# A chunked scan joined to a gated feed-forward layer: a new order for the scan of the last three chunks, the sums for the seven products, and own tiles for the last rows

## The chip, the cores and the metric

One core of a Trainium2 chip runs the whole kernel in one launch. The metric is device time in microseconds (us), the median of repeated executions. TensorE (PE) multiplies matrices, with its weight loads (PEld) shown apart; VectorE (DVE), ScalarE (ACT) and GpSimd (POOL) work element by element; SyncE (SP) issues most DMA transfers. Each engine works through its own list of instructions in order; semaphores are all that ties one list to another.

## The reference, cut to what matters

```python
# x (4, 8, 768, 32), a (4, 8, 768), B and C (4, 8, 768, 16); float32
for c in chunks:                                   # state-space scan
    cum = cumsum(log(clip(a)))
    M = (C @ B.T) * exp(cum_i - cum_j) * causal
    y = M @ x + (C @ state) * exp(cum)
    state = exp(sum(log a)) * state + sum_j B_j x_j exp(cum_last - cum_j)
z = y.transpose(0, 2, 1, 3).reshape(3072, 256)     # all heads side by side
gate = sigmoid(z @ w_gate)                         # 256 x 1536
out = (gate * (z @ w_val)) @ w_out                 # 1536 x 256
```

The kernel walks the sequence in six chunks of 128 positions. The 512 rows of `z` that belong to one chunk (four batches) go through the feed-forward layer as soon as the scan has made them.

## The kernel before, in words

Products in single precision are made of three products of rounded parts: an operand is cast to a high part, and the difference to the operand is the low part. So every operand costs a cast (mostly ACT) and a subtraction (mostly POOL or DVE), named hi and lo below.

For chunks 0 to 3 the feed-forward layer runs as `gateK_f` and `valueK_f` (K the chunk, f one of 12 strips): six matmuls of 128x512 each (line 1244) into PSUM tiles `pg` and `pv`, a sigmoid on ACT, a multiplication on DVE (line 1205), then hi (line 1209) and lo (line 1211). `projK` (line 1500) multiplies by the output weights, in two column halves 0 and 1. Three PSUM banks serve all of these.

Chunks 4 and 5 are joined. Their rows and the weights are cut in two by two blocks, and seven products stand for eight (the "scheme of seven products"). It needs sums of rows (`x_block`: names b11, b21, b22, t1 to t4) and, for each of 12 weight tiles, sums of weights (`s_block`, s0 to s11: one sum `ww`, four sums `sw`, hi, lo). `group` i does the seven products (line 1365, 3 matmuls each, tiles gva, gvb, gvd). `corner` takes them out of PSUM (copy on ACT, line 1398; sums on DVE, line 1400; sigmoid; multiplication, lines 1391 and 1407). `h_parts` makes hi (line 1417) and lo (line 1419) of the result. `out` multiplies by the output weights (line 1441). `stored_rows` copies and stores the results (lines 1455 and 1457).

The scan of chunks 2 to 5 runs in ten pieces, `block0` to `block9`, that lie between the steps of the feed-forward layer on PE. A block makes the part across chunks for one half of the batches, the products of B and C for a later half, and the part within the chunk for the half between. After a block, ACT copies the banks (`inner`), DVE weighs the products (`weights`), adds (`result`) and forms the states (`after`); the next block needs these.

What stands where is written out by hand: `ORDER` is a list of steps, each an engine and a task, and `run` issues exactly that list, so it sets the order on each engine. A step's needs are only tested against that list; they do not move anything.

Of the kernel before, what the change touches and what calls it, by code (L numbers as in the profile page):

```python
# [88 lines left out]
pool.value2_2 sp.x4_2 dve.value2_3 pe.gate2_4 sp.b5_2 dve.after3_2 sp.p4_0 act.value2_3 dve.after3_2
pe.value2_4 act.gate2_4 pool.value2_3 sp.a5_2 dve.value2_4 pe.gate2_5 dve.turn4_2 act.value2_4 pe.value2_5  # L90
act.gate2_5 pool.value2_4 sp.t5_0 act.turn4_2 dve.value2_5 pe.gate2_6 act.value2_5 pe.value2_6 act.gate2_6
pool.value2_5 pool.before4_0 dve.value2_6 pe.gate2_7 sp.p4_2 dve.decays5_2 act.value2_6 sp.a5_3 pe.value2_7
act.gate2_7 pool.value2_6 dve.value2_7 pe.gate2_8 dve.turn5_0 act.value2_7 pe.value2_8 act.gate2_8
pool.value2_7 sp.t5_2 act.turn5_0 dve.value2_8 pe.gate2_9 dve.decays5_3 act.value2_8 pe.value2_9 act.gate2_9
pool.value2_8 dve.value2_9 pe.gate2_10 act.value2_9 pe.value2_10 act.gate2_10 pool.value2_9 pe.block5
dve.value2_10 act.value2_10 pool.value2_10 pe.gate2_11 act.inner4_0 dve.weights4_2 sp.x5_0 pool.before4_2
dve.after4_0 dve.weights4_2 pool.decays5_0 act.gate2_11 pe.value2_11 dve.result3_2 pool.decays5_1 dve.after4_0
act.result3_2 dve.turn5_2 pool.result3_2 pe.proj2_0 dve.after4_0 act.turn5_2 dve.value2_11 dve.after4_0
act.value2_11 dve.result3_2 pe.proj2_1 dve.after4_0 pool.value2_11 act.result3_2 dve.after4_0 sp.p5_0
pool.result3_2 pe.proj2_0 pe.proj2_1 pe.proj2_0 pe.proj2_1 dve.proj2_0 pe.gate3_0 dve.proj2_1 sp.proj2_1  # L100
# [12 lines left out]
act.xb22_1 pe.block8 dve.xb22_0 pool.xb22_1 dve.value3_11 dve.value3_11 pe.proj3_0 dve.result5_0
pool.value3_11 act.inner5_2 dve.result5_0 dve.xb11_0 pool.xt1_0 act.xb21_0 pe.proj3_0 dve.xb11_0 dve.xb21_0
pool.xt2_0 act.xt1_0 dve.xt1_0 pe.proj3_1 act.xt2_0 dve.xt4_0 pool.xt3_1 dve.xt2_0 act.xt4_0 dve.xt4_0 pool.s0
act.xt3_1 pe.proj3_1 dve.xt3_1 dve.after5_2 dve.after5_2 dve.after5_2 dve.s0 pe.block9 pe.proj3_0
dve.result5_2 act.s0 dve.result5_2 pe.proj3_0 dve.xb11_1 pool.s0 act.xb21_1 dve.xb11_1 dve.xb21_1 pe.proj3_1
dve.xt1_1 dve.xt2_1 act.xt1_1 dve.xt2_1 pool.xt4_1 dve.xt2_1 pe.proj3_1 dve.xt1_1 act.xt4_1 dve.xt4_1 dve.s1
pool.s2 pe.group0 dve.s1 pe.group0 act.corner0_11 pe.group0 act.s1 dve.s2 pe.group0 act.corner0_22 dve.s1
act.corner0_21 pe.group0 dve.corner0_11 pool.s3 act.s2 pe.proj3_0 dve.corner0_21 act.corner0_11 dve.s2  # L120
act.corner0_21 pe.group0 dve.s3 pe.proj3_0 dve.corner0_22 act.s3 dve.proj3_0 pe.group0 act.corner0_22 pool.s3
pe.group1 act.corner0_12 pe.group1 act.corner1_11 pe.group1 act.corner1_22 pe.group1 dve.corner1_11 pe.group1
act.corner1_21 dve.corner1_11 pe.proj3_1 dve.corner1_21 dve.corner1_21 pe.group1 pe.proj3_1 dve.corner1_22
dve.corner1_22 pe.group1 act.part0_11 dve.proj3_1 pool.s4 pe.group2 act.part0_22 pe.group2 dve.part0_11
# [74 lines left out]
def tile_ssd_then_gated_ffn(  # L199
# [1109 lines left out]
    def s_block(i):  # L1309
# [4 lines left out]
        if i == 0:  # L1314
            needs += [("py", 2 * T1 + 1)]
# [532 lines left out]
```

## Time and profile before

| | |
|---|---|
| median of 3 runs | 366.8 us (365.11 to 366.99) |
| the profiled execution | 366.27 us |
| its span, first to last instruction | 364.5 us |
| PE busy | 346.8 us, 95% of the span |
| DVE, ACT, POOL busy | 241.2, 168.3, 178.0 us |
| granted TensorE clock, mean | 0.998 |

The profiled execution is 1.77 us longer than its span. A busy PE is not a PE at its peak, since the ends of matmuls are modelled: the pace is better read from the distance between the starts of like steps. The feed-forward layers of chunks 1 to 3 and the blocks of the scan take PE from about 88 to 235 us, the joined chunks from there to the end.

### The profile page before, as it was taken

The numbers are of one execution on the slowest core, as the hardware profiler recorded it, in microseconds if no ns is written. First come the engines' busy times: TensorE is split into PE (matmuls) and PEld (weight loads), VectorE is DVE, ScalarE is ACT, GpSimd is POOL, SyncE is SP. The second block draws the span as 40 slices with busy tenths as digits, with TensorE's granted clock in tenths as the row PEclk, the third lists the DMA queues.
The fourth block names the chain that finished last, engine by engine and source line by source line (L and its number), as shares of the span: only waits on it lengthen the run. The fifth ranks groups of instructions, "written<-read, shape, count | busy, mean of one in ns | idle before, by whom it ended". The sixth has DMA issues, their size and how long they took to land.

```text
span 364.5 us, 8267 instructions
## 1 busy us (share of the span) xinstructions
PE 346.8 (95%) x3328; PEld 277.5 (76%) x3328; DVE 241.2 (66%) x425; ACT 168.3 (46%) x315; POOL 178.0 (49%) x174
## 2 busy tenths in 40 slices
PE   8999999999999999999999999978999798999993
PEld 3567477787888888888888888856788686888883
DVE  7787688776428775545611234789798979666473
ACT  2585784356875410555310443323646363534521
POOL 6444875746898642456520454455415656313030
PEclk9999999999999999999999999999999999999999
DMA  7999964445364434253200210000011000000003
GB/s 166 242 231 212 335 185 134 107 84 94 107 117 127 80 84 90 58 101 103 45 14 13 49 30 12 8 0 2 1 32 28 0 0 2 0 2 0 0 2 115
DMA packets 87467, 27.43 MB, mean 75 GB/s; under 512 B 75718, under 2 KB 80262, under 8 KB 87430
## 3 DMA queue, kind: packets, MB, share of 16 engines
q1 hardware_dynamic: 82982, 26.26, 30.4%
q10 hardware_dynamic: 4448, 0.66, 1.1%
q8 instruction: 26, 0.43, 0.5%
q14 instruction: 11, 0.09, 0.1%
HBM read 23.46 MB, written 3.44 MB: 74 GB/s over the span
## 4 chain that ended last, share of the span: by engine, by line
PE 63%; DVE 18%; DMA 5%; SPq 4%; issue 3%; ACT 1%; POOL 0%; DVEq 0%; POOLq 0%
PE pg L1244 13%; PE pv L1244 13%; PE po L1500 10%; PE po L1538 6%; PE acc L1441 5%; PE gva L1365 4%; DVE c L1400 3%; DVE c L1407 3%; PE gvb L1365 3%; DVE h L1417 2%; PE gvd L1365 2%; DMA a_z<-a 2%; DMA wr<-in_moe_w_val_dram 2%; SPq L418 2%; PE banks L784 1%
## 5 line engine op out<-in xcount | busy, mean ns | idle before, releaser
L1211 POOL TENSOR_TENSOR h<-g,h 128x512 fp32r<-128x512 f32 x36 | 48.8, 1357 | 57.4 <-ACT h L1209 55.6
L1244 PE MATMUL pg<-xh,w 128*128 128x512 f32 x168 | 59.6, 395 | 0.0
L1244 PE MATMUL pv<-xh,w 128*128 128x512 f32 x168 | 58.9, 391 | 0.1
L1205 DVE TENSOR_TENSOR g<-pv,g 128x512 f32<-128x512 f32 x36 | 24.8, 689 | 40.4 <-PE pv L1244 39.2
L1500 PE MATMUL po<-h,w 128*128 128x512 f32 x216 | 50.9, 391 | 0.0
L1500 PEld LDWEIGHTS po<-h,w 128*128 128x128 f32 x216 | 40.3, 188 | 8.6
L1441 PEld LDWEIGHTS acc<-w,h 128*128 128x128 f32 x288 | 38.7, 190 | 3.4 <-DVE h L1419 0.4
L1441 PE MATMUL acc<-w,h 128*128 128x256 f32 x288 | 40.0, 283 | 0.2 <-DVE h L1419 0.2
L1419 POOL TENSOR_TENSOR h<-c,h 128x512 fp32r<-128x512 f32 x11 | 19.0, 1741 | 43.2 <-ACT h L1417 29.7
L1184 ACT ACTIVATE g<-pg 128x512 f32<-128x512 f32 x44 | 26.3, 598 | 29.3 <-PE pg L1244 28.9
L1209 ACT CAST h<-g 128x512 fp32r<-128x512 f32 x35 | 21.7, 619 | 37.9 <-DVE g L1205 37.9
L1244 PEld LDWEIGHTS pg<-xh,w 128*128 128x128 f32 x168 | 31.5, 188 | 7.9 <-DVE h L1201 0.8
L1244 PEld LDWEIGHTS pv<-xh,w 128*128 128x128 f32 x168 | 31.5, 188 | 7.2 <-POOL w L496 0.6
L1244 PE MATMUL pg<-xl,w 128*128 128x512 f32 x84 | 32.7, 390 | 0.0
L1244 PE MATMUL pv<-xl,w 128*128 128x512 f32 x84 | 32.7, 389 | 0.0
L574 DVE TENSOR_TENSOR_SCAN ab<-ab,delta 128x512 f32<-128x512 f32 x20 | 28.0, 1403 | 4.1 <-DMA ab<-a_z 4.1
L496 POOL TENSOR_TENSOR w<-wr,w 128x512 fp32r<-128x512 f32 x18 | 26.7, 1485 | 7.8 <-ACT w L494 7.0
L477 POOL TENSOR_TENSOR wr<-wr 128x512 int32<-128x512 int32 x18 | 20.4, 1138 | 12.6 <-ACT wr L475 7.7
L1538 PE MATMUL po<-wr,h 128*128 128x256 f32 x96 | 23.4, 394 | 0.1
L1332 POOL TENSOR_TENSOR s<-sw,s 128x512 fp32r<-128x512 f32 x8 | 10.8, 1362 | 22.8 <-ACT s L1330 22.8
L1538 PEld LDWEIGHTS po<-wr,h 128*128 128x128 f32 x96 | 17.6, 188 | 4.3 <-DVE h L1201 0.6
L1400 DVE TENSOR_TENSOR c<-gva,c 128x512 f32<-128x512 f32 x12 | 8.3, 690 | 18.8 <-PE gva L1365 18.7
(194 smaller groups left out, 669.2 us busy)
## 6 DMA issues: line engine op xcount, KB each, us to landing
ab<-a_z SPq DMA_DIRECT2D x40, 128.0 KB
wr<-in_moe_w_gate_dram SPq DMA_DIRECT2D x6, 512.0 KB
wr<-in_moe_w_val_dram SPq DMA_DIRECT2D x6, 512.0 KB
wr<-in_moe_w_out_dram SPq DMA_DIRECT2D x6, 512.0 KB
xn<-in_x_dram SPq DMA_DIRECT2D x10, 256.0 KB
out_dram<-o SPq DMA_DIRECT2D x48, 32.0 KB
bn<-in_B_dram SPq DMA_DIRECT2D x10, 128.0 KB
out_dram<-o SPq DMA_DIRECT2D x10, 128.0 KB
```

The source lines that it names most:

```text
L477: nc.gpsimd.tensor_tensor(out=lw.bitcast(I32), in0=hw.bitcast(I32), in1=lw.bitcast(I32), op=ALU.add)
L496: engines[eng].tensor_tensor(out=lo, in0=lw, in1=hi.bitcast(F32), op=ALU.subtract)
L574: nc.vector.tensor_tensor_scan(out=t.rearrange("p h l -> p (h l)"), data0=t.rearrange("p h l -> p (h l)"), data1=delta.rearrange("p h l -> ...
L1184: nc.scalar.activation(gs[k, f], pm, AF.Sigmoid)
L1205: nc.vector.tensor_tensor(out=g, in0=pm, in1=g, op=ALU.mult)
L1209: copies[eng](hh, g)
L1211: engines[eng].tensor_tensor(out=hl, in0=g, in1=hh.bitcast(F32), op=ALU.subtract)
L1244: nc.tensor.matmul(pm, w[:, part, kt, fs], xx[:, kt], start=(i == 0), stop=(i == 3 * NK - 1))
L1365: nc.tensor.matmul(out, one, two, start=m == 0 and n in (1, 7, 2), stop=m == 2, skip_group_check=True)
L1441: nc.tensor.matmul(acc[:, k * DM : (k + 1) * DM], one(js), w[:, two, :], start=first and m == k == 0, stop=final and m == 2, skip_group_ch ...
L1500: nc.tensor.matmul(acc, w[:, part], hs[k, f][:, of_h], start=(f == 0 and i == 0), stop=(f == NF - 1 and i == 2))
L1538: nc.tensor.matmul(acc[:, :DM], hs[k, f][:, js], whole[NF + f // 2][:, f % 2], start=start, stop=stop, skip_group_check=True,)
```

## The change

`ORDER` is new from the middle of chunk 1 on. Blocks 2 to 9 stand earlier: block 6 moves from chunk 3's strips into those of chunk 2, block 7 to their end, and blocks 8 and 9 from the joined chunks' stage into `proj2`. The sums of x for t1 to t4 follow in `proj2` and at the start of chunk 3; b22 and s0 to s3 stand within chunk 3's strips; s4 to s7 during `proj3` and `group0`. Four weight sums, s8 to s11, stay among the groups. In `h_parts` the cast is always on ACT. `proj3` takes strips 8 to 11 first, which sets free the tiles that s4 to s7 use. The last four rows of chunk 5 get two more buffers, of the tag "cd". No arithmetic is added or taken away; the number of PE instructions is the same.

```diff
 ORDER = """
...
-pe.gate3_10 act.value3_9 pe.value3_10 act.gate3_10 pool.value3_9 dve.value3_10 pe.gate3_11 dve.after5_0
+pe.proj2_1 pool.xt1_0 pool.xt2_0 act.xt1_0 pool.xt1_0 act.xt2_0 pool.xt2_0 pe.block9 pe.proj2_0 pool.xt4_0
...
@@ x_block
-        needs += [("gv", T2 - 1)] if MOVING_LAST[name] else []
+        needs += {"b1": [("gv", T2 - 1), ("t1", 0)], "b2": []}.get(name[:2] if name != "b21" else "b1", [("gv", T2 - 2)] if name in ("t1", "t2") else [])
...
@@ s_block
-        needs = [("w", i), ("gv", T2 - 1)] + ([("s7", i - 2)] if i > 1 else [])
...
-        needs += {0: moved if v else [], 1: moved, 2: [("proj", T2 - 1)], 3: [("proj", T2 - 1)], 4: [("done", 1)], 5: [("done", 2)]}[j]
+        needs = [("w", i)] + ([("sums", i - 1)] if i else [])
+        needs += {
+            0: [("py", 2 * T1 + 1)], 1: [("py", 2 * T1 + 1)], 2: moved, 3: moved, 4: [("projf", 8)], 5: [("projf", 8)],
+            6: [("projf", 10)], 7: [("projf", 10)], 8: [("done", 2)], 9: [("done", 3)], 10: [("done", 4)], 11: [("done", 5)],
+        }[i]
...
@@ h_parts
-        eng = yield step(("act", "dve"), (ACT_SB, DVE_MM), [("hf", j, n)] + ([("hused", j - 2, n)] if j > 1 else [("proj", T2 - 1)]))
+        eng = yield step("act", ACT_SB, [("hf", j, n)] + ([("hused", j - 2, n)] if j > 1 else [("proj", T2 - 1)]))
...
@@ stored_rows
-            pool, tag = (wk, "o") if k == T1 else (ld, ("bn", "pp")[at])
+            pool, tag = (wk, ("o", "cd")[at]) if k == T1 else (ld, ("bn", "pp")[at])
...
@@ proj_turned
-        for n in range(0, NF, size):
+        starts = [*range(8, NF, 2), *range(0, 8, 2)] if size == 2 else [*range(0, NF, 4)]
+        for n in starts:
...
-                        acc, w[:, part], hs[k, f][:, of_h], start=(f == 0 and i == 0), stop=(f == NF - 1 and i == 2)
+                        acc, w[:, part], hs[k, f][:, of_h], start=f == starts[0] and i == 0,
+                        stop=f == starts[-1] + size - 1 and i == 2,
```

On PE, block 9 before (the eight rows with `banks` and `local`) stands within `proj3`, after strips 0 to 3 of both halves (`po_0`, `po_1`; `h_3` and `h_4` are strips):

```order
L1500 MATMUL po_1_3129<-h_3_2679,w_1269 128x512 x3
L814 MATMUL banks<-cd_2_2983,sn_2865 64x64 x3
L814 MATMUL local<-cd_2_2983,sn_2865 64x64
L814 MATMUL banks<-cd_2_2983,sn_2865 64x64 x3
L814 MATMUL local<-cd_2_2983,sn_2865 64x64
L814 MATMUL banks<-cd_2_2983,sm_3157 64x64 x3
L814 MATMUL local<-cd_2_2983,sm_3157 64x64
L814 MATMUL banks<-cd_2_2983,sm_3157 64x64 x3
L814 MATMUL local<-cd_2_2983,sm_3157 64x64
L1500 MATMUL po_0_3098<-h_4_2699,w_1358 128x512 x3
```

In the changed kernel the same block, at its new line, stands within `proj2`, between strips 7 and 8, with chunk 3's strips still to come:

```order
L1506 MATMUL po_1_2715<-h_7_2495,w_1399 128x512 x3
L815 MATMUL banks<-cd_2_2700,sn_2530 64x64 x3
L815 MATMUL local<-cd_2_2700,sn_2530 64x64
L815 MATMUL banks<-cd_2_2700,sn_2530 64x64 x3
L815 MATMUL local<-cd_2_2700,sn_2530 64x64
L815 MATMUL banks<-cd_2_2700,sm_2811 64x64 x3
L815 MATMUL local<-cd_2_2700,sm_2811 64x64
L815 MATMUL banks<-cd_2_2700,sm_2811 64x64 x3
L815 MATMUL local<-cd_2_2700,sm_2811 64x64
L1506 MATMUL po_0_2684<-h_8_2544,w_1452 128x512 x3
```

So the block moved ahead of twelve strips of chunk 3 and of all of `proj3`.

On DVE, this is what stands before between the weight sums of s6 and the next ones, at the end of group 3 (`c2` and `c3` are the corners of groups 2 and 3, `h1` the second pair's result):

```order
L1400 TENSOR_TENSOR c3_11_3483<-gva_3234,c3_11_3483 128x512
L1407 TENSOR_TENSOR c2_11_3392<-c3_11_3483,c2_11_3392 128x512
L1400 TENSOR_TENSOR c3_21_3508<-gvd_3235,c3_21_3508 128x512
L1407 TENSOR_TENSOR c2_21_3421<-c3_21_3508,c2_21_3421 128x512
L1400 TENSOR_TENSOR c3_22_3491<-gvb_3236,c3_22_3491 128x512
L1407 TENSOR_TENSOR c2_22_3402<-c3_22_3491,c2_22_3402 128x512
L1417 CAST h1_22_3545<-c2_22_3402 128x512
L1419 TENSOR_TENSOR h1_22_3545<-c2_22_3402,h1_22_3545 128x512
L1391 TENSOR_TENSOR c2_12_3473<-gvb_3236,c2_12_3473 128x512
L1417 CAST h1_12_3568<-c2_12_3473 128x512
L1419 TENSOR_TENSOR h1_12_3568<-c2_12_3473,h1_12_3568 128x512
```

The changed kernel has this at the same place, after the sums of s8:

```order
L1404 TENSOR_TENSOR c3_11_3501<-gva_3290,c3_11_3501 128x512
L1411 TENSOR_TENSOR c2_11_3428<-c3_11_3501,c2_11_3428 128x512
L1404 TENSOR_TENSOR c3_21_3530<-gvd_3291,c3_21_3530 128x512
L1404 TENSOR_TENSOR c3_22_3514<-gvb_3292,c3_22_3514 128x512
L1411 TENSOR_TENSOR c2_22_3438<-c3_22_3514,c2_22_3438 128x512
L1423 TENSOR_TENSOR h1_11_3543<-c2_11_3428,h1_11_3543 128x512
L1423 TENSOR_TENSOR h1_22_3569<-c2_22_3438,h1_22_3569 128x512
L1395 TENSOR_TENSOR c2_12_3494<-gvb_3292,c2_12_3494 128x512
L1423 TENSOR_TENSOR h1_12_3590<-c2_12_3494,h1_12_3590 128x512
```

Both casts went to ACT and the multiplication of corner 21 to POOL; the lo of part 11 came from POOL to DVE.

On POOL, this piece of chunk 3's strips before holds nothing but the strips' own lo (`h_4`, `h_5`, `h_6`) and the scan's small products:

```order
L1211 TENSOR_TENSOR h_4_2699<-g_4_2688,h_4_2699 128x512
L1211 TENSOR_TENSOR h_5_2792<-g_5_2708,h_5_2792 128x512
L584 TENSOR_TENSOR bd_2_2808<-bn_1_2182,ab_2_2201 128x128
L584 TENSOR_TENSOR bd_3_2811<-bn_1_2182,ab_3_2273 128x128
L856 TENSOR_TENSOR cd_0_2822<-bct_0_2294,pp_0_2524 128x256
L1211 TENSOR_TENSOR h_6_2839<-g_6_2824,h_6_2839 128x512
```

In the changed kernel chunk 3's strips on POOL have weight sums (`ww`), a lo of weight sums (`s_1`) and the lo of b22 (`xb`) among them:

```order
L1212 TENSOR_TENSOR h_3_3014<-g_3_3001,h_3_3014 128x512
L1297 TENSOR_TENSOR xb_3016<-y_0_2243,xb_3016 128x2x2x64
L1297 TENSOR_TENSOR xb_3016<-y_2_2506,xb_3016 128x2x2x64
L1212 TENSOR_TENSOR h_4_3040<-g_4_3027,h_4_3040 128x512
L1324 TENSOR_TENSOR ww_3061<-w_1101 128x512
L1212 TENSOR_TENSOR h_5_3063<-g_5_3050,h_5_3063 128x512
L1212 TENSOR_TENSOR h_6_3088<-g_6_3072,h_6_3088 128x512
L1336 TENSOR_TENSOR s_1_3110<-sw_3083,s_0_3100 128x512
L1212 TENSOR_TENSOR h_7_3112<-g_7_3097,h_7_3112 128x512
```

The scan's small products moved to chunk 2 and before, and larger work took their place.

## Rows read from the trace of the kernel before

**Rows 1.** Busy time by stretch: start:end, length, then each engine's busy us.

```profile
88.00:125.20 37.20, 37.20 (x434) 30.41 (x434) 21.82 (x34) 25.32 (x43) 29.47 (x23) 1.00 0.53 110
...
234.70:262.10 27.40, 23.29 (x232) 18.30 (x232) 24.59 (x54) 10.70 (x22) 13.03 (x13) 1.00 0.01 1
262.10:313.00 50.90, 47.19 (x259) 40.56 (x258) 43.81 (x78) 26.31 (x46) 25.99 (x18) 1.00 0.05 11
313.00:345.50 32.50, 31.65 (x181) 27.46 (x181) 20.41 (x28) 14.39 (x25) 6.94 (x4) 1.00 0.00 1
345.50:358.90 13.40, 13.03 (x88) 11.45 (x86) 9.69 (x13) 3.59 (x8) 3.54 (x2) 1.00 0.04 14
```

**Rows 2.** Waits of PE: us in total, times, the longest in us.

```profile
PE gvb L1365 <- DVE c L1391: 4.1, 4, 1.8
PE local L814 <- DVE ml L676: 2.4, 1, 2.4
```

**Rows 3.** Timeline of PE from 236 to 266: start, length, engine, line, work.

```profile
236.21 5.73 PE L1500 MATMUL po<-h,w 128*128 128x512 f32 x24
241.87 0.34 PE L814 MATMUL banks<-cd,sn 32*64 32x64 f32 x6
244.57 0.27 PE L814 MATMUL local<-cd,sn 32*64 32x64 f32 x1 [2.36 <-DVE ml L676]
...
245.36 5.76 PE L1500 MATMUL po<-h,w 128*128 128x512 f32 x24
...
252.99 0.84 PE L1365 MATMUL gva<-xt,s 128*128 128x512 f32 x3
255.28 0.96 PE L1365 MATMUL gvd<-xt,w 128*128 128x512 f32 x3 [1.44 <-ACT c L1398]
...
264.17 1.52 PE L1500 MATMUL po<-h,w 128*128 128x512 f32 x6
265.53 0.84 PE L1365 MATMUL gvb<-xt,s 128*128 128x512 f32 x3
```

**Rows 4.** Timeline of PE where group 3 ends and group 4 begins.

```profile
281.62 1.59 PE L1441 MATMUL acc<-w,h 128*128 128x256 f32 x12
283.04 0.95 PE L1365 MATMUL gvb<-xb,s 128*128 128x512 f32 x3
...
285.19 0.87 PE L1441 MATMUL acc<-w,h 128*128 128x256 f32 x6
287.84 0.96 PE L1365 MATMUL gvb<-x,w 128*128 128x512 f32 x3 [1.78 <-DVE c L1391]
```

**Rows 5.** Timeline of DVE, at 236 us and where group 3 ends.

```profile
236.94 0.43 DVE L1209 CAST h<-g 128x512 fp32r<-128x512 f32 x1
...
284.11 1.40 DVE L1417 CAST h<-c 128x512 fp32r<-128x512 f32 x1
285.54 1.65 DVE L1419 TENSOR_TENSOR h<-c,h 128x512 fp32r<-128x512 f32 x1
287.11 0.68 DVE L1391 TENSOR_TENSOR c<-gvb,c 128x512 f32<-128x512 f32 x1
```

**Rows 6.** Timeline of POOL over the same place.

```profile
281.77 3.45 POOL L1419 TENSOR_TENSOR h<-c,h 128x512 fp32r<-128x512 f32 x2
285.19 3.13 POOL L1320 TENSOR_TENSOR ww<-w 128x512 f32<-128x512 f32 x2
```

**Rows 7.** A strip of chunk 3: PE's last product and POOL's lo.

```profile
231.74 0.39 PE L1244 MATMUL pv<-xh,w 128*128 128x512 f32 x1
```

**Rows 8.** Timeline of POOL, the lo of that strip.

```profile
233.66 1.29 POOL L1211 TENSOR_TENSOR h<-g,h 128x512 fp32r<-128x512 f32 x1 [1.43 <-ACT h L1209]
```

**Rows 9.** Timeline of all engines at the end.

```profile
352.92 5.97 PE L1441 MATMUL acc<-w,h 128*128 128x256 f32 x46 [0.22 <-DVE h L1419]
...
358.67 0.36 ACTq L1457 DMA_DIRECT2D out_dram<-o  x1
...
361.37 0.42 DVE L1455 COPY o<-acc 128x256 f32<-128x256 f32 x1 [2.01 <-DMA out_dram<-o]
```

More of the change, by code (lines that the diff above doesn't have):

```diff
@@ L153 @@
+pe.out3_21 pe.group9 dve.corner9_22 pe.group10 dve.corner9_12 pool.part4_21 act.part4_22 pe.group10
+act.corner10_11 pe.out4_11 dve.part4_22 act.part4_12 pe.group10 act.corner10_22 dve.part4_12 pe.group10
 dve.corner10_11 pe.group10 act.corner10_11 pe.out4_11 act.corner10_21 pe.group10 dve.corner10_21 pe.out4_22
@@ L1267, in x_block @@
         needs = [("sum", p) for p in ((p2,) if name in ("b22", "t3") else (p1,))]
-        needs += [("gv", T2 - 1)] if MOVING_LAST[name] else []
+        needs += {"b1": [("gv", T2 - 1), ("t1", 0)], "b2": []}.get(name[:2] if name != "b21" else "b1", [("gv", T2 - 2)] if name in ("t1", "t2") else [])
+        if name == "b22":
+            needs.append(("out", T2 - 2))
+        if name == "t3":
+            needs += [("pcd", 2 * T1), ("pcd", 2 * T1 + 1)]
         if name in ("t1", "t3"):
@@ L1283, in x_block @@
             needs = []
-        eng = yield step(("act", "dve"), (ACT_HALF, DVE_HALF), needs)
+        eng = yield step(("act", "dve"), (ACT_HALF, DVE_HALF), needs, port=True)
         src = sums(name) if name[0] == "t" else (y2 if name == "b22" else y1)(int(name[1] == "2"))
@@ L1320, in s_block @@
         engines[eng].tensor_tensor(out=ww, in0=w[:, 0].bitcast(F32), in1=w[:, 1].bitcast(F32), op=ALU.add)
-        yield step("dve", 4 * 0.28, port=True)
+        yield step("dve", 4 * 0.28, [("s7", i - 1)] if i else [], [("sums", i)], port=True)
         t = ld.tile([P, 4, P], F32, tag="ab", name=f"sw{i}", bufs=NDEC)
@@ L1355, in group @@
                 needs += [("sum", 2 * T1 + 1), ("pfirst", 2 * T1 + 1)]
-            made = [("p", n, i)] + ([("done", i // 2)] if n == (4 if i == NF - 1 else 3) and i % 2 else [])
+            made = [("p", n, i)] + ([("done", i)] if n == (4 if i == NF - 1 else 3) else [])
             yield step("pe", 3 * 0.227, needs, made, port=12)
@@ L1488, in proj_turned @@
         size = 2 if k + 1 in JOINED else 4
-        for n in range(0, NF, size):
+        starts = [*range(8, NF, 2), *range(0, 8, 2)] if size == 2 else [*range(0, NF, 4)]
+        for n in starts:
             some = range(n, n + size)
-            needs = [("h", k, f) for f in some] + sorted({("w", NF + f // 2) for f in some}) + ([] if n else [("gv", k)])
-            yield step(
-                "pe", size * 3 * 0.227, needs, [("proj", k)] if mt and n + size == NF else [], port=24, banks=int(n == 0)
-            )
-            if n == 0:
+            needs = [("h", k, f) for f in some] + sorted({("w", NF + f // 2) for f in some})
+            needs += [("gv", k)] if n == 0 and size == 4 else []
+            makes = [("projf", n)] if mt and size == 2 else []
+            makes += [("proj", k)] if mt and n == starts[-1] else []
+            yield step("pe", size * 3 * 0.227, needs, makes, port=24, banks=int(n == starts[0]))
+            if n == starts[0]:
                 acc = ps_mm.tile([P, 512], F32, tag="mm", name=f"po{k}_{mt}")
```

186 lines of the change are left out of this document (91 added, 95 removed).

## The prediction, made before the run

> **What bounds the kernel now.** I read the busy time by stretch first, then the waits of PE, then the timelines around the longest of these waits. PE sets the pace from 88 us on. In the strips of chunk 1 it is busy for all of 37.20 us, with two blocks of the scan among them. After 234.70, where the last strip of chunk 3 ends, it idles 4.11 us of 27.40, then 3.71 of 50.90, 0.85 of 32.50 and 0.37 of 13.40, 9.04 in sum [rows 1]. So what an order can win lies in the joined chunks, and the reader is to see who ends those waits. The two longest entries name DVE [rows 2]. DVE is busy for 24.59 of 27.40 us and 43.81 of 50.90 in the two stretches with much waiting, and for 20.41 of 32.50 in the one with little [rows 1]. DVE's timeline shows why it is so full: a cast that takes 0.43 us at 236.94 takes 1.40 at 284.11, and a subtraction after it 1.65 [rows 5], while POOL works without a break from 281.77 to 288.32 [rows 6]. The two slow each other where both work on SBUF alone.
>
> **The change part by part.** PE's instructions stay the same, so I count lost time from start to start, which also holds PE's slow start after a stop.
>
> Block 9 waits within proj3: its first matmuls start at 241.87, the next at 244.57, so 2.7 us are lost to one small multiplication (ml) queued on DVE behind the sums of x [rows 3]. That block moves into proj2, where no sums of x stand on DVE. Gain 2.7.
>
> In group 0 the fourth product starts at 252.99. A product of three matmuls takes half of what six of the same shape take, (265.53 - 264.17) / 2 = 0.68, so the next could start at 253.67; it starts at 255.28 [rows 3]. Loss 1.6, from x and weight sums made on the spot. A third stop in this stretch is 4.11 - 2.36 - 1.44 = 0.3 [rows 1, 3]. With x's sums and s0 to s3 done in chunk 3's strips, both go: 1.9.
>
> At the ends of groups 1, 3, 5, 7 and 9 the third product of the next group needs a bank that DVE frees with the corner's multiplication (line 1391). At group 3 the last two output steps take 1.42, so 0.71 each; the step at 285.19 is over at 285.90, the product starts at 287.84, a loss of 1.9 [rows 4] of which 1.8 is told as wait. The four such waits are 4.1 [rows 2], and all idling between 262.10 and 345.50 is 3.71 + 0.85 = 4.6 [rows 1]. With some 0.15 us (1.94 - 1.78) of slow start at each of about six stops, 5.5 is lost here. At the end of group 3 DVE spends 1.40 + 1.65 on a cast and a subtraction before it reaches that multiplication at 287.11 [rows 5]. Now both casts are on ACT, and four weight sums instead of eight lie among the groups. What stays, by the new order and the rows' lengths: from the product that DVE's last sum needs to the product that waits, PE has two output steps, three products and an output step, 2 x 0.71 + 3 x 0.68 + 0.71 = 4.2. In that time DVE has the sum, one multiplication, two subtractions and the corner's multiplication, 5 x 0.68 = 3.4. That leaves 0.8, so one collision with an operation of POOL (1.29, [rows 8]) costs 0.5 and two cost 1.8. I take 0.3 at the end of group 1, where a transposition of proj3 stands in between, 0.4 at 3 and 5, where POOL works too, and nothing at 7 and 9, where the corner's multiplication comes ahead of the subtractions: 1.1 stays, between 0 and 5.5. Gain 4.4.
>
> In the last two pairs' end PE idles 0.37 [rows 1], with slow starts some 0.6; the casts of the last parts leave DVE. I take 0.4 of it.
>
> After the last matmul: PE ends at 352.92 + 5.97 = 358.89. The last copy starts at 361.37 behind the landing of an earlier store, since four rows share two buffers, and ends at 361.79; from there 2.7 us pass to the end of the span at 364.50 [rows 9]. With own buffers ACT goes on from its store at 358.67: that store 0.36, a copy 0.42, a store 0.36, a copy 0.42, so the last copy ends at 360.23 [rows 9], 1.6 earlier. If the stores' landing, and not the last copy, sets the end, the gain is less, down to 0.5.
>
> Now what is added. First, proj3 begins with strips 8 and 9 and asks for strip 11 after two steps of 1.36, 2.7 us. In a strip of chunk 3 PE starts its last product at 231.74, so is free 0.23 later at 231.97 (a sixth of 1.36), and POOL ends the lo at 233.66 + 1.29 = 234.95 [rows 7, 8]: 3.0 later. Before, strips 0 to 7 came first and hid that. Cost 0.3 to 1.6 (one more POOL operation in front); I take 0.4.
>
> Second, eight blocks (2 to 9) now ask for their inputs earlier, and DVE's scans and transpositions, and the loads on SP's queue, move with them. The cover is that blocks 1 and 2 stand among strips without any idle PE [rows 1], and that before only one block shows a wait [rows 2]. In the new order the closest pair is blocks 7 and 8, two steps of proj2 apart, 24 matmuls, which took 241.87 - 236.21 = 5.7 us [rows 3], in which DVE has two weighings, two results and three small operations, some 4 us by rows like 0.68 [rows 5]. The price lies between 0 and 2.7 per block, 21.6 in all; nearest to the rows is 0, and I take 0.4 in all. The new sums are queued behind these on DVE and POOL and are needed much later.
>
> Third, POOL in chunk 3's strips (12 x 2.72 = 32.6 us): eleven lo of 1.29, four more operations of that size and five of half size, 14.2 + 5.2 + 3.8 = 23.2 us [rows 8], 71%. In chunk 1's strips POOL is busy 29.47 of 37.20, 79%, and PE never waits [rows 1]. DVE adds three subtractions of 0.68 and sixteen small sums there. Cost 0 to 3, taken as 0.3. s4 to s7 between proj3's steps and group 0: 0 to 2, taken as 0.3.
>
> The sum: 2.7 + 1.9 + 4.4 + 0.4 + 1.6 - 0.4 - 0.4 - 0.3 - 0.3 = 9.6. From the profiled execution's own 366.27 that gives 356.7. The median of the runs lies 0.5 above it, so I predict 357.0 (range of this case 351 to 361).
>
> A rule of the Trainium skill speaks against a part of this. "SBUF — State Buffer", section "Who interferes with whom", says that a DVE operation with two SBUF inputs, or a cast in a two-port mode, and a GpSimd operation that reads SBUF shut each other out for a whole instruction, whoever starts first. The trace agrees in kind (1.40 for 0.43, above). By that rule the subtractions that came to DVE can each wait for a whole operation of POOL, at any of the five ends of groups; what that would give is the first rival.
>
> **The rivals.** (1) The ends of groups stay slow. The lo of part 11 came to DVE and the multiplication of corner 21 to POOL, so two collisions can still fall into each of these ends, and s4 to s7 run against POOL's lo of x. Then the 4.4 is not won and s4 to s7 cost 1 more: 357.0 + 4.4 = 361.4, with a part of it some 360.5. For it: 1.65 for a subtraction [rows 5]. Against: POOL has fewer operations there, and the stretch without weight sums loses only 0.85 in 32.50 [rows 1].
>
> (2) Slower: the pulled-ahead scan makes PE wait at each block, because `inner`, `weights` and `after` of one block must be through before the next, now at closer distance, with value multiplications in between. Place: PE's `banks` and `local` in chunks 1 and 2. At block 9's price of 2.7 for eight blocks it costs 21.6, of which 0.4 is in the sum already: 357.0 + 21.2 = 378. From (9.8 + 1.8) / 8, about 1.5 us per block, the kernel is slower by more than 0.5%; a centre is 372. For it: that one price was paid [rows 3]. Against: it was paid where DVE was full, and DVE is busy 21.82 of 37.20 where two blocks wait for nothing [rows 1].
>
> (3) No gain: the waits only move, since DVE, POOL and ACT have the same work in all. The 9.04 of idling then reappears in proj2, chunk 3's strips or group 0: about 366 with the own buffers' 1.6 partly kept. Against: chunk 3's strips have free DVE time.
>
> **How the numbers follow.** The forecast has 0.62, rival (1) 0.21, rival (2) 0.10, rival (3) 0.07. A measurement of this kernel tells about 0.5%, 1.8 us, from no change. Faster by more than that (under 365.0): 0.62 + 0.21 = 0.83; within it: 0.07; slower: 0.10. The range runs from 351.0 (all of 2.7 + 1.9 + 5.5 + 0.6 + 1.6, with no cost, and 3 x (32.50 - 0.85 - 2 x (14 x 0.68 + 8 x 0.71)) = 3.8, what three such stretches lose beyond their steps and stops [rows 1]) to 364.8: it takes in rival (1) and leaves out (2), (3) and the rare better case, under 0.2.
>
> **What would show it.** Right: PE without idle time from 88 us past the last strip of chunk 3; `local` without a wait for ml; group 0 without a stop; line 1391's four waits (now at 1395) together under 1.5; no DVE cast in the parts of the last stage; last copy within 1.5 us of the last matmul. Wrong: waits of `banks` for `m` or `y`, `pg` or `pv` waiting for ACT or DVE in chunk 3, or stops at every second group end as long as before.

## The result: 356.05 us against 366.83, and the profile after

The changed kernel takes 356.05 us (median of six runs, 355.48 to 356.60), the kernel before 366.83 in the same comparison; the ratio is 0.9714, 95% interval 0.9693 to 0.9735. The forecast was 357.0, range 351.0 to 364.8. The profiled execution takes 356.60 us, its span 354.7, the granted clock 0.998.

Where the 9.8 us of span went is best read from starts that both traces have. "Step of group i" is the time from its second product (tile gvd, first written) to that of the next group.

| stretch of PE | before | changed | gain | by the prediction's terms |
|---|---|---|---|---|
| span's start to block 1's first `local` | 94.82 | 95.77 | -0.95 | 0 |
| from there to group 0's first product | 156.13 | 154.20 | 1.93 | 2.7 - 0.4 - 0.4 - 0.3 = 1.6 |
| step of group 0 | 9.82 | 7.48 | 2.34 | 1.9 - 0.3 = 1.6 |
| steps of groups 2, 4, 6, 8, 10 (group 1's end, and so on) | 45.07 | 40.22 | 4.85 | 4.4 |
| steps of groups 1, 3, 5, 7, 9 | 38.31 | 38.23 | 0.08 | 0 |
| from group 11's second product to the last matmul's end | 14.06 | 13.97 | 0.09 | 0.4 |
| from there to the span's end | 5.61 | 4.15 | 1.46 | 1.6 |

The first row is not the change: that stretch took 94.67 to 97.24 us in the thirteen traces of this study. From block 1 on the gain is 10.75, which fits the medians (366.83 - 356.05 = 10.8).

Busy time by stretch of the changed kernel (columns as in [rows 1]); the last three lines are the joined chunks without their end:

```profile
88.00:125.20 37.20, 36.32 (x458) 29.08 (x457) 26.79 (x40) 24.32 (x44) 28.59 (x26) 1.00 0.59 127
206.40:239.00 32.60, 32.60 (x145) 26.99 (x145) 15.94 (x32) 16.59 (x29) 21.08 (x19) 1.00 0.08 17
239.00:266.00 27.00, 27.00 (x121) 22.36 (x120) 20.11 (x37) 11.66 (x22) 6.04 (x7) 1.00 0.00 1
266.00:313.00 47.00, 46.35 (x268) 40.49 (x268) 32.32 (x57) 27.41 (x47) 15.87 (x11) 1.00 0.06 12
313.00:347.00 34.00, 33.86 (x205) 29.98 (x203) 19.23 (x29) 17.11 (x30) 4.13 (x3) 1.00 0.00 1
```

Chunk 3's strips carry the sums without any idle PE, with DVE and POOL at 49% and 65%. `proj3` and group 0 have none either. What idles is 0.65 + 0.14 us in the joined chunks, and 0.88 in chunk 1, which was fully busy before. The waits of PE say who ends these (as in [rows 2]; from 88 us on):

```profile
PE pg L1245 <- DVE g L1206: 0.9, 1, 0.9
...
PE gvb L1369 <- DVE c L1395: 0.6, 2, 0.4
...
PE acc L1445 <- DVE h L1423: 0.2, 1, 0.2
```

`local` no longer waits, and the four waits of 4.1 in all are two of 0.6 in all. Both are at the ends of groups 3 and 5. (Before, the four lie at the ends of groups 3, 5, 7 and 9; the end of group 1, which the prediction counts too, has none.) PE there, for [rows 4]:

```profile
281.42 0.84 PE L1369 MATMUL gvd<-xt,s 128*128 128x512 f32 x3
282.10 0.87 PE L1445 MATMUL acc<-w,h 128*128 128x256 f32 x6
283.35 0.96 PE L1369 MATMUL gvb<-x,w 128*128 128x512 f32 x3 [0.37 <-DVE c L1395]
```

DVE and POOL there, for [rows 5, 6]:

```profile
280.31 2.38 DVE L1423 TENSOR_TENSOR h<-c,h 128x512 fp32r<-128x512 f32 x2
282.61 0.68 DVE L1395 TENSOR_TENSOR c<-gvb,c 128x512 f32<-128x512 f32 x1
```

```profile
280.57 1.57 POOL L1423 TENSOR_TENSOR h<-c,h 128x512 fp32r<-128x512 f32 x1 [0.73 <-ACT h L1421]
282.10 1.73 POOL L1324 TENSOR_TENSOR ww<-w 128x512 f32<-128x512 f32 x1
```

The casts are gone from DVE's chain. The two subtractions that are left take 2.38; a pair of them with POOL idle takes 1.30 (at 346.30). The corner's multiplication behind them reads one operand from PSUM and takes its 0.68 while POOL works.

The new stop in chunk 1, DVE first:

```profile
95.36 1.73 DVE L857 TENSOR_TENSOR cd<-bct,pp 128x256 f32<-128x256 f32 x1
97.00 2.31 DVE L575 TENSOR_TENSOR_SCAN ab<-ab,delta 128x512 f32<-128x512 f32 x1
99.24 0.26 DVE L677 TENSOR_TENSOR ml<-local,mask 128x128 f32<-128x128 f32 x1
99.61 1.85 DVE L755 SCALAR_TENSOR_TENSOR sm<-sq,pp,ml 128x64 f32<-128x64 f32 x2
...
102.18 0.68 DVE L1206 TENSOR_TENSOR g<-pv,g 128x512 f32<-128x512 f32 x1
```

```profile
102.91 0.50 PE L1245 MATMUL pg<-xh,w 128*128 128x512 f32 x1 [0.88 <-DVE g L1206]
```

Two steps that came forward in the order (`before2_0` from POOL to DVE, and the scan of `decays3_0`) hold DVE for 4 us, and the strip's multiplication, which frees a bank, is late. At the end of the kernel, for [rows 9]: the last matmuls start at 347.65 and end at 350.55, ACT's last copy starts at 351.53, 0.98 later, and waits for no landing. So of the signs that I had named only the first failed in part: PE does idle between 88 us and the end of chunk 3, once.

One part of the change is in no account so far: the sums changed engine as well as place. Of the 36 steps of `ORDER` that make the sums of x, DVE had 21 and POOL 5; now DVE has 1 and POOL 22. Of the 48 for weight sums DVE had 18 and POOL 18; now it is 26 and 10. In the kernel before, line 1292 alone (the lo parts of x) holds DVE for 7.19 of the 16 us from 240 on (columns DVE and POOL):

```profile
240.00:256.00 16.00, 7.19 (x10) 0.00 (x0) 1.00 0.00 1
```

### The profile page after: what moved, and what is told of

The parts are those of the page before. It is cut to its first block, busy times and chain, and to the rows that moved or that the text cites. A ratio compares the mean times of both kernels' runs of the same rounds, so it can differ in the third digit from the quotient of the medians.

```text
span 354.7 us, 8271 instructions
## 1 busy us (share of the span) xinstructions
PE 345.0 (97%) x3328; PEld 277.1 (78%) x3328; DVE 230.5 (65%) x405; ACT 175.1 (49%) x330; POOL 170.3 (48%) x179
## 4 chain that ended last, share of the span: by engine, by line
PE 64%; DVE 4%; ACT 1%; POOL 1%; issue 1%; ACTq 0%; DVEq 0%; POOLq 0%
PE po L1506 14%; PE pg L1245 13%; PE pv L1245 12%; PE acc L1445 6%; PE gva L1369 6%; PE gvb L1369 5%; PE gvd L1369 4%; PE banks L785 1%; DVE c L1404 1%; DVE h L1423 1%; PE banks L769 1%; ACT h L1421 1%; PE banks L815 1%; POOL c L1411 1%; DVE c L1411 1%
## 5 line engine op out<-in xcount | busy, mean ns | idle before, releaser
L1212 POOL TENSOR_TENSOR h<-g,h 128x512 fp32r<-128x512 f32 x35 | 47.4, 1356 | 36.5 <-ACT h L1210 35.2
L497 POOL TENSOR_TENSOR w<-wr,w 128x512 fp32r<-128x512 f32 x18 | 25.8, 1437 | 7.5 <-ACT w L495 7.1
L575 DVE TENSOR_TENSOR_SCAN ab<-ab,delta 128x512 f32<-128x512 f32 x20 | 27.1, 1374 | 2.3 <-DMA ab<-a_z 2.3
L1423 POOL TENSOR_TENSOR h<-c,h 128x512 fp32r<-128x512 f32 x7 | 11.4, 1646 | 35.5 <-ACT h L1421 35.5
L1421 ACT CAST h<-c 128x512 fp32r<-128x512 f32 x24 | 14.7, 622 | 16.4 <-DVE c L1411 13.0
## 6 DMA issues: line engine op xcount, KB each, us to landing
ab<-a_z SPq DMA_DIRECT2D x40, 128.0 KB
bn<-in_B_dram SPq DMA_DIRECT2D x10, 128.0 KB
out_dram<-o SPq DMA_DIRECT2D x9, 128.0 KB
```

The lines of the kernel that those rows point to most:

```text
L497: engines[eng].tensor_tensor(out=lo, in0=lw, in1=hi.bitcast(F32), op=ALU.subtract)
L575: nc.vector.tensor_tensor_scan(out=t.rearrange("p h l -> p (h l)"), data0=t.rearrange("p h l -> p (h l)"), data1=delta.rearrange("p h l -> ...
L1212: engines[eng].tensor_tensor(out=hl, in0=g, in1=hh.bitcast(F32), op=ALU.subtract)
```

## The experiments

All are timed beside the kernel before, five rounds. Besides the ratio I compare the stretches of the table, since the first 95 us vary by more than most effects. In these kernels lines have lower numbers, since `ORDER` takes fewer lines: the corner's multiplication is L1387 (L1383 or L1384 where `needs` lines went too), not L1395.

**Own buffers for the last rows, undone.**

```diff
-            pool, tag = (wk, ("o", "cd")[at]) if k == T1 else (ld, ("bn", "pp")[at])
+            pool, tag = (wk, "o") if k == T1 else (ld, ("bn", "pp")[at])
```

> The changed kernel, but the last four rows of chunk 5 share the two buffers of tag "o" again; the order stays. My theory (own buffers set the last copies free, worth about 1.5 us): the last copies wait for the landing of earlier stores, the span grows from 354.7 to about 356.2, the median from 356.05 to about 357.5, and from the last matmul to the end pass some 5.6 us instead of 4.15. Rival (the new order of copies and stores at the end made the gain, or the landing of the last store sets the end anyway): under 0.5 us more.

Ratio 0.9764 (0.9729 to 0.9800). From the last matmul to the end pass 5.52 us, not 4.15: some 1.4 more, as the spans are told to 0.1. The median, 358.51, lies 1.0 above the 357.5 that I expected; the six runs spread from 356.80 to 361.12, and in the profiled one the first stretch took 97.24 us, 1.47 more than in the changed kernel's trace. Two copies wait for a landing again, ACT's is this:

```profile
354.74 0.38 ACT L1451 COPY o<-acc 128x256 f32<-128x256 f32 x1 [1.91 <-DMA out_dram<-o]
```

The term is the buffers'.

**Casts back on DVE** (eight steps of `ORDER`).

```diff
-pe.out0_21 pe.group3 ... act.part1_22 pe.group4 dve.part1_22 ... act.part1_12 dve.part1_12
+pe.out0_21 pe.group3 ... dve.part1_22 pe.group4 dve.part1_22 ... dve.part1_12 dve.part1_12
```

> The changed kernel, but the casts of parts 22 and 12 of groups 2 to 9 (parts 1 to 4, eight casts) go back to DVE at the same places of the order. My theory (DVE's path to the corner's multiplication is what PE waits for at the ends of groups 3 and 5, and a cast lengthens it by 0.43 to 1.40 us): the wait of gvb grows from 0.6 us by 0.9 to 2.8, all of it at groups 3 and 5, nothing at 7 and 9 where the multiplication stands ahead of the casts; the median goes to 357.0 to 358.9. Rival (the ends became fast because weight sums left them, the casts are hidden): under 0.4 us more.

Ratio 0.9800 (0.9770 to 0.9830). The steps of groups 4 and 6 grow from 8.32 and 8.19 to 9.74 and 9.62, those of 8 and 10 by 0.07 each: 2.99 in all, a little over the upper end of 2.8, and where my theory had it. The median, 359.67, is over its range too. DVE at the end of group 3, and PE's wait:

```profile
280.48 0.68 DVE L1415 TENSOR_TENSOR h<-c,h 128x512 fp32r<-128x512 f32 x1
281.08 1.51 DVE L1413 CAST h<-c 128x512 fp32r<-128x512 f32 x1
282.63 1.65 DVE L1415 TENSOR_TENSOR h<-c,h 128x512 fp32r<-128x512 f32 x1
284.20 0.68 DVE L1387 TENSOR_TENSOR c<-gvb,c 128x512 f32<-128x512 f32 x1
```

```profile
PE gvb L1361 <- DVE c L1387: 3.4, 2, 1.8
```

**Weight sums s4 to s11 back among the groups**, casts still on ACT. They also go back to the engines they had: eight of their steps from DVE to POOL.

```diff
-... pe.proj3_0 dve.s4 pe.proj3_1 dve.s4 pool.xb11_1 act.s4 pe.proj3_0 dve.s4 dve.s5 ...
+... dve.proj3_1 pool.s4 pe.group2 ... pool.s5 act.corner2_11 ... dve.s5 act.corner2_22 pe.group2 pe.group3 dve.s6 ...
```

> The changed kernel, but the weight sums s4 to s11 stand among the groups again, at the places they had before; the casts stay on ACT. My theory gives the casts about two thirds of what the ends of groups won (about 4.3 us) and the sums one third: 0.5 to 2.0 us more, median 356.6 to 358.0. Rival (the weight sums made the ends slow): 3 to 4 us more, 359 to 360, with waits of gvb at groups 1, 3, 5 as long as before. A third case (sums cost nothing anywhere, DVE has room): no change.

Ratio 0.9803 (0.9775 to 0.9831), some 3.3 us over the changed kernel, which is the rival's figure. The waits of gvb at groups 3 and 5, 1.55 and 1.31, are nearly those of the kernel before (1.78 and 1.49); at group 1 there is none, but the kernel before has none there either. So my share of two thirds for the casts fell. DVE's pair of subtractions at the end of group 3 grows from 2.38 to 3.47, beside three operations of POOL in a row, and PE's slow stretch behind the stop comes on top (last line, PEclk 0.58):

```profile
280.18 3.47 DVE L1411 TENSOR_TENSOR h<-c,h 128x512 fp32r<-128x512 f32 x2
```

```profile
279.67 1.75 POOL L1312 TENSOR_TENSOR ww<-w 128x512 f32<-128x512 f32 x1
281.37 1.73 POOL L1411 TENSOR_TENSOR h<-c,h 128x512 fp32r<-128x512 f32 x1
283.07 1.71 POOL L1312 TENSOR_TENSOR ww<-w 128x512 f32<-128x512 f32 x1
```

```profile
284.31 1.42 PE L1357 MATMUL gvb<-x,w 128*128 128x512 f32 x3 [1.55 <-DVE c L1383]
285.53 1.48 PE L1357 MATMUL gva<-xt,s 128*128 128x512 f32 x3
```

```profile
284.00:288.00 4.00, 3.69 (x9) 2.93 (x10) 3.10 (x10) 1.51 (x3) 0.78 (x1) 0.58 0.00 0
```

So casts and sums are not two shares of one gain. Each alone brings back a stop.

**All sums late, blocks early.** Additionally the sums of x and s0 to s3 stand where they stood, on the engines they had, and `proj3` takes strips 0 to 11 in order.

> The changed kernel, but all sums of x and of weights stand where they stood before (in proj3, group 0 and among the groups), and proj3 takes its strips in the order 0 to 11 again; blocks 2 to 9 stay early, the casts stay on ACT, the last rows keep their buffers. My theory (the stops in group 0 come from sums made on the spot): as with s4 to s11 alone late, plus about 1.9 us in group 0, and no wait of local at a block, so 358.5 to 360. Rival (DVE is full in that stretch only because the scan's last blocks stood there too): group 0 stays without a stop, no more than with s4 to s11 alone late.

Ratio 0.9944 (0.9922 to 0.9967), median 365.41: over 8 us more than the changed kernel, far past my 358.5 to 360. The stretch to group 0 stays short (154.20), but the step of group 0 takes 14.97, where the kernel before needs 9.82: the first seven products wait 1.22 and 2.92, and then the granted clock falls (the two middle lines, column PEclk: means of 0.58 and 0.57; 0.5 is 1.2 GHz). The rival, no stop in group 0, fell with it:

```profile
252.00:256.00 4.00, 1.43 (x5) 0.51 (x4) 3.90 (x8) 0.89 (x2) 2.10 (x2) 1.00 0.00 0
256.00:260.00 4.00, 2.43 (x6) 1.95 (x7) 3.97 (x9) 2.21 (x4) 1.27 (x1) 0.58 0.01 2
260.00:264.00 4.00, 4.00 (x12) 3.13 (x11) 2.27 (x7) 1.94 (x5) 1.08 (x1) 0.57 0.00 0
264.00:268.00 4.00, 4.00 (x19) 3.26 (x19) 1.19 (x2) 2.23 (x4) 2.71 (x3) 1.00 0.00 0
```

DVE is busy for 3.90 and 3.97 of 4.00 us in the first two. This gave the idea for the next run.

**The kernel before, block 9's wait taken away.** Three steps move.

```diff
-act.inner5_2 dve.result5_0 dve.xb11_0 ... dve.xt3_1 dve.after5_2 dve.after5_2 dve.after5_2 dve.s0
+act.inner5_2 dve.result5_0 dve.after5_2 dve.after5_2 dve.after5_2 dve.xb11_0 ... dve.xt3_1 dve.s0
```

> The kernel before, with one thing changed: the three state steps that block 9 waits for stand ahead of the sums of x on DVE. My first theory (the 2.7 us of block 9's wait are a term of their own): that wait goes and the rest stays, 2.7 us less, ratio 0.993. New theory (after the run with all sums late: the sums of x and of the first weights take DVE a fixed time after chunk 3, and whatever PE does not wait for in proj3 it waits for in group 0): local's wait goes, group 0 starts up to 2.7 earlier and its first seven products take as much longer; ratio 0.998 to 1.004.

Ratio 1.0020 (1.0002 to 1.0039). The wait of `local` is gone, and group 0's first product comes after 153.07 us instead of 156.13; its step takes 14.34 instead of 9.82. All 3.06 are given back, and 1.6 more, as the new theory has it and not the first. At the fifth product, the last one that waits, PE stands 160.18 us behind block 1, and 160.46 in the kernel before: the waits alone take back 2.8. The rest comes behind that product, with the clock down again (0.84 and 0.50 here):

```profile
252.42 0.96 PE L1358 MATMUL gva<-xt,s 128*128 128x512 f32 x3 [0.86 <-ACT c L1391]
256.32 1.65 PE L1358 MATMUL gvd<-xt,w 128*128 128x512 f32 x3 [2.94 <-ACT c L1391]
```

```profile
252.00:256.00 4.00, 0.96 (x3) 0.48 (x3) 3.90 (x9) 1.20 (x3) 1.65 (x2) 0.84 0.00 0
256.00:260.00 4.00, 3.68 (x9) 2.91 (x10) 3.97 (x10) 2.60 (x5) 0.48 (x1) 0.50 0.00 0
```

**The kernel before, all casts of the last stage's parts on ACT** (eleven steps, `dve.partJ_nn` to `act.partJ_nn`).

> The kernel before, with all casts of the last stage's parts on ACT, at the same places. If DVE's path at the ends of groups is casts and stretched subtractions together: the waits of gvb at groups 3 and 5 fall by one stretched cast each, 0.9 to 2.8 us less in all, and nothing changes before group 1. Rival (the weight sums on POOL stretch what is left as much): under 0.6 us less.

Ratio 0.9944 (0.9925 to 0.9964), 2.1 us less, within the first theory's range. The steps of groups 4, 6, 8 and 10 fall by 0.62, 0.65, 0.29 and 0.29, the stretch behind the last group's second product by 0.46; groups 2 and 3 rise by 0.41. The waits of gvb shrink to one of 0.4, but two of gva for ACT's copy (2.0 us) come in their place, as the casts now stand in ACT's list. Against the forecast, this profile also differs before group 1: the clock fell behind block 9's wait (0.54 from 244 to 248), group 0 came 2.8 later, and its step was 7.49, without a stop.

```profile
PE gva L1358 <- ACT c L1391: 2.0, 2, 1.0
PE gvb L1358 <- DVE c L1384: 0.4, 1, 0.4
```

```profile
244.00:248.00 4.00, 3.33 (x32) 2.73 (x33) 3.89 (x14) 1.02 (x2) 1.21 (x1) 0.54 0.00 0
```

The edit touches nothing before group 0's parts, so this is no effect of it. Of the 42 executions of the kernel before that were timed beside these experiments, 41 had a mean granted clock of 0.983 to 0.993 and one had 0.998. The trace behind the prediction, at 0.998, is of the rare kind, and what a lower clock takes in the others is in none of its rows.

**Two steps of the scan in chunk 1 moved in the changed kernel**: `before2_0` back to POOL, `decays3_0` behind strip 4's multiplication.

```diff
-pool.value1_1 dve.before2_0 dve.decays3_0 act.part14 ... pool.decays3_0 dve.after2_0 pe.value1_2
+pool.value1_1 pool.before2_0 act.part14 ... pe.value1_2
-dve.value1_4 dve.value1_4 pool.part16 pe.value1_5
+dve.value1_4 dve.value1_4 dve.decays3_0 pool.part16 pool.decays3_0 pe.value1_5
```

> The changed kernel, but the products before2_0 of the scan go back to POOL, and the scan step decays3_0 on DVE moves behind the multiplication of strip 4 of chunk 1 (its POOL step with it). My theory (the stop of 0.9 us at strip 1 of chunk 1 comes from these two on DVE, 1.73 and 2.31 us for what takes 0.42 and 1.21 alone): pg's wait for the multiplication goes, and strips to group 0 take 0.9 to 1.0 us less from the first block's start: 160.7 instead of 161.70; ratio about 0.969. Rival (DVE is late there whatever stands in the list, or block 2 waits for the later step): no change or a new wait of a block.

Ratio 0.9672 (0.9650 to 0.9695). The wait is gone, and from block 1 to group 0 pass 153.25 us, 0.95 less. Which of the two steps did it is not separated.

**The corner's multiplication first at the ends of groups 3 and 5.**

```diff
-dve.part1_22 act.corner4_11 pe.out1_11 dve.corner3_12
+dve.corner3_12 act.corner4_11 pe.out1_11 dve.part1_22
```

> The changed kernel, but at the ends of groups 3 and 5 the corner's multiplication stands ahead of the second subtraction on DVE. My theory (that multiplication alone holds PE): the two waits of gvb (0.6 us in 2) go, the groups 4 and 6 take some 0.5 and 0.4 us less, 0.9 in all, ratio about 0.969. Rival: the output steps then wait for the subtraction that is now late, and the gain is under 0.3 or none.

Ratio 0.9678 (0.9654 to 0.9702). The steps of groups 4 and 6 are 7.69 and 7.69, 1.13 less in all, and no output step waits for the later subtraction. The subtractions take 0.68 and 1.17, together 1.85 instead of 2.38, and PE's product no longer stands behind the second:

```profile
281.91 0.69 DVE L1387 TENSOR_TENSOR c<-gvb,c 128x512 f32<-128x512 f32 x1
282.52 1.17 DVE L1415 TENSOR_TENSOR h<-c,h 128x512 fp32r<-128x512 f32 x1
```

**The changed kernel again**, for comparison with the next two.

> The changed kernel once more, beside the others on the same chip, so that they can be compared with it: ratio 0.9714 as before, within its interval.

356.33 us, ratio 0.9699 (0.9676 to 0.9721).

**The first sums of s9 and s11 on DVE**, inside groups 4 and 6.

```diff
-dve.corner4_11 pool.s9 act.corner4_21 ... pe.group4 dve.s9 act.corner4_21
+dve.corner4_11 act.corner4_21 ... pe.group4 dve.s9 dve.s9 act.corner4_21
```

> The changed kernel, but the first sums of s9 and s11 (128x512 on POOL, 1.73 us at the ends of groups 3 and 5) are made on DVE, later, within groups 4 and 6. My theory (DVE's two subtractions take 2.38 us there, not 1.37, because POOL works beside them): without the POOL sum they take some 1.9, and the waits of gvb at the ends of groups 3 and 5 (0.37 and 0.21) shrink to nothing; the steps of groups 4 and 6, 8.32 and 8.19, fall by 0.3 to 0.6 each, 0.6 to 1.1 us less in all. Rival (DVE's list is too long there, whatever POOL does): the waits stay, and DVE's extra 0.68 makes groups 4 and 6 slower by up to 0.5 each.

Ratio 0.9724 (0.9699 to 0.9749), and my expectation fell. The pair still takes 2.38, the wait is still 0.38, and the steps of groups 4 and 6 grow by 0.55 and 0.53, as the rival said of the added work (with two new waits of `gva` for DVE, 0.27 each):

```profile
280.30 2.38 DVE L1415 TENSOR_TENSOR h<-c,h 128x512 fp32r<-128x512 f32 x2
282.61 0.68 DVE L1387 TENSOR_TENSOR c<-gvb,c 128x512 f32<-128x512 f32 x1
```

```profile
280.57 1.57 POOL L1415 TENSOR_TENSOR h<-c,h 128x512 fp32r<-128x512 f32 x1 [0.73 <-ACT h L1413]
```

The extra 1.1 us of the pair comes beside POOL's lo of part 21 alone. POOL's weight sum began at 282.10, when the pair was nearly through; there POOL was the one to be stretched (1.73). No run takes that lo away, so that it makes the 1.1 is read from the traces and not shown by an edit.

**Four edits of the order together:** the two above that gained; ACT's copy ahead of the sigmoid in group 2; the last copy on DVE.

```diff
-act.corner2_11 pe.out0_11 act.corner2_21 pe.group2
+act.corner2_21 pe.out0_11 act.corner2_11 pe.group2
-sp.rows5_1 act.rows5_0 act.rows5_1 act.rows5_1
+sp.rows5_1 act.rows5_0 dve.rows5_1 act.rows5_1
```

> The changed kernel with four edits of the order: the two on the scan in chunk 1 (0.95 us less, measured alone), the corner's multiplication first at the ends of groups 3 and 5 (1.13 less), ACT's copy for the third corner ahead of the sigmoid in group 2 (its step is 8.13 against 7.69 elsewhere: 0.2 to 0.4 less), and the last copy on DVE beside ACT's (0.4 less after the last matmul). If the terms add, 2.7 to 2.9 us less than the changed kernel, median about 353.3, ratio 0.9635 to 0.9645; if they don't (a stop moves to the next place), at least 1 us of it is missing.

354.20 us, ratio 0.9643 (0.9618 to 0.9668); the five runs lie between 353.14 and 354.82, the four of the changed kernel beside it between 356.23 and 356.38. The ratio is within the forecast's 0.9635 to 0.9645; by the medians the gain is 2.13, less than the 2.7 to 2.9. In the profiled execution, the fastest of the five, the span from block 1 on is 2.60 shorter than the changed kernel's: 1.07 up to group 0, 1.14 at groups 4 and 6, 0.35 in group 2, and nothing that can be told from zero at the end. This version beats both. From block 1 on PE has one wait over 0.15 us, of 0.22, and the first three edits' terms add. Only the last copy earned nothing: on DVE it starts earlier, but ACT's last two stores still end 1.45 behind the last matmul and the span 2.64 behind them:

```profile
347.51 0.85 ACTq L1453 DMA_DIRECT2D out_dram<-o  x2
```

## Why the prediction was right, and where it was not

**Block 9's wait and the sums (2.7 and 1.9).** Together they gave 1.93 + 2.34 net. But they are not two terms, as the prediction had it; that is the step of it that failed. Taking the wait alone out of the kernel before won nothing: group 0 took it back. From block 1 to group 1's second product the kernel before needs 156.13 + 0.68 + 9.82 = 166.6 us; with the wait gone, 153.07 + 0.80 + 14.34 = 168.2; with blocks early and all sums late, 154.20 + 0.68 + 14.97 = 169.9; with PE slowed at block 9, 158.92 + 0.68 + 7.49 = 167.1. DVE is busy for 97% of the 16 us from 240 to 256 in the kernel before, and what PE saves it waits for later:

```profile
240.00:256.00 16.00, 12.20 (x80) 9.42 (x79) 15.56 (x35) 5.21 (x12) 7.69 (x7) 1.00 0.00 1
```

Only with the sums moved out too does it become 162.4. Moved out means two things here, earlier and, for the sums of x, from DVE to POOL; no run does one without the other, so which of them was needed stays open. Rival (3), the waits only move, describes what the block's move alone does; its premise, that DVE, POOL and ACT have the same work in all, holds for the three together and not for each. The prediction held since the change does both; that its two separate terms add up to a right sum is luck.

**Costs of what moved (0.4 + 0.4 + 0.3 + 0.3).** Strip 11's lo, POOL in chunk 3 and s4 to s7 cost nothing that a wait of PE shows; three terms of 1.0 in all were too careful. POOL was busy for 21.08 us in chunk 3's strips, where 23.2 was reckoned. The eight blocks cost 0.95 instead of 0.4, shown by moving two steps away. The price was paid by a strip's multiplication behind them on DVE. Rival (2) looked at the block's own waits, and none appeared. The cover that I named (DVE busy for 21.82 of 37.20 with two blocks) was an average: 6.8 us of DVE's operations in a row (95.36 to 102.18) in front of one multiplication made the stop.

**Ends of groups (4.4).** 4.85 measured: 1.90 and 1.75 at groups 3 and 5, 0.76 each at 7 and 9, and 0.32 lost at group 1 (7.81 became 8.13). The 1.1 that stays was predicted as 0.3, 0.4 and 0.4 at groups 1, 3 and 5. Measured by the runs that remove them: 0.35 at group 1, 0.63 and 0.50 at 3 and 5. At group 1 it is not DVE, as I had it, but an ACT copy behind a sigmoid, and it is no remainder: the kernel before has the copy first there, and the change turned the two round. So that 0.3 came out right by luck. That one POOL operation meets the subtractions at 3 and 5, at 0.5 us each, was the right mechanism. What I could not tell is that neither the casts nor the sums alone would have done: with either one back, stops of 1.3 to 1.8 are back. Casts alone moved to ACT gain 2.1.

**What stretches the subtractions.** The Trainium skill, "SBUF — State Buffer", section "Who interferes with whom", says that a DVE operation with two SBUF inputs contends with a GpSimd operation that reads SBUF, that one with at most one, outside the two-port modes, does not, and that issue order decides who waits. The traces here agree: two SBUF inputs 2.38 for 1.30, one PSUM input 0.68 beside POOL and without it. On a whole operation's lock they differ a little: an estimate by that rule is 1.30 + 1.29 = 2.59 for the pair, the trace has 2.38. Rival (1), which took the rule at its worst at every end, did not come about.

**Last pair (0.4) and own buffers (1.6).** 0.09 and 1.46. Of the first, both stops of before are still there: one of 0.14 at 341.79, which waits for a corner's sum on DVE and costs 0.31 from start to start, and one of 0.23 at 347.65, behind the last subtraction. The term was of the right size for the casts: with them alone on ACT the kernel before won 0.46 here and lost the stop behind the subtraction. But the change also moved the last pair's two lo of POOL to DVE, which makes two in a row (1.30 from 346.30), and the one that PE needs first stands second. That this took the gain back is read from the lists; no run moves them back. The buffers' term is confirmed by undoing it (some 1.4).

By size, from block 1 on, the change won 10.75 where 9.6 was forecast, and by the medians 10.8. The 0.95 that the first 95 us took back in the profiled execution is not in the medians. In the prediction's own sums, 9.6 from a median of 366.8 is 357.2 and not 357.0, and rival (1) names 1 us more for s4 to s7 that its 361.4 leaves out; neither changes what was forecast.

What stays open: why the granted clock falls behind some stops and not behind others of the same length. It fell after the 2.4 us of block 9's wait in one trace (0.54) and stayed at 1.00 after the same wait in the kernel before. At the end of group 3 it fell behind a stop of 1.55 with the weight sums late and stayed at 1.00 behind one of 1.56 with all sums late.

## What to carry to other kernels

When an engine is full over a stretch, a wait of PE in it is not a term by itself: take away the work, or PE meets the same queue one stage later. For each operation that PE waits for, count what stands directly in front of it on its engine, at the lengths that the trace has beside POOL, and put the one that frees a bank first. A busy share over 37 us hides 6 us in a row.

## What the runs showed of the hardware

- The slow stretch after a stop can cost as much as the stop. With the weight sums late, the step of group 4 took 11.33 us, with a stop of 1.55 and then 4 us at a mean granted clock of 0.58; with all sums late the same step, behind a stop of 1.56, stayed at 1.00 and took 9.82. The lower clock alone is 1.5 us. The kernel before has a stop of 1.78 there and stays at 1.00.
- DVE's scan over 128x512, beside POOL, took 2.31 us, for 1.21 at 128.0, where POOL began only later, and a pair of small multiplications with three operands 1.85, for 0.47 later in the same strip.
- The span ends 2.4 to 2.6 us after the last store was issued, in the changed kernel and in the version with four edits alike; ending the last copy 0.56 earlier behind the last matmul (0.80 for 1.36) did not shorten the end by more than 0.1.
